# Weight sizes by column sums on TensorE instead of reductions on VectorE, with redrawn scheduling priorities

## The chip, the cores and the metric

The kernel runs on one core of a Trainium2 chip. The metric is the device time of one execution in microseconds; the median of several runs counts. Engines are named as in the profile: PE (TensorE, matmuls), PEld (its weight loads), DVE (VectorE), ACT (ScalarE), POOL (GpSimd), SP (SyncE, which issues all DMAs here).

## The reference

The inputs are a sequence x of 2048 rows and 448 columns, four square weights wq, wk, wv, wo (448x448), w1 (448x1792), w2 (1792x448), a gate vector and 16 values beta. Two branches are mixed row by row:

```python
g = sigmoid((x * gate_w).sum(-1, keepdims=True))
# branch a, 16 heads of 28, 4 segments s of 512 rows, memory M, z from zero
p = softmax(qs @ ks.T * scale + mask); a_dot = p @ vs        # causal in a segment
a_mem = (phi(qs) @ M) / (phi(qs) @ z + 1e-6)                 # phi(t) = t+1 if t>0 else exp(t)
o = sigmoid(beta) * a_mem + (1 - sigmoid(beta)) * a_dot
M = M + phi(ks).T @ vs; z = z + sum(phi(ks))
a = concat(o) @ wo
b = silu(x @ w1) @ w2
out = g * a + (1 - g) * b
```

## The kernel before, in words

**Number formats.** Each operand of a product is split into a high part and the remainder, and three products of parts stand for one. Projections use fp32r parts, everything later f16 parts. To stay in range, f16 operands are multiplied by powers of two that come from the size of a tensor. So the kernel measures sizes: of each segment of x, of wv, of wq and wk, of two 64-column halves of a block of w1 that ride along in the packed wq and wk (HQ, HK), of w1, w2 and wo.

**How a size is taken.** `size` (L378) lets VectorE reduce a loaded piece to one maximum of absolute values for each partition (L385). `scales` (L396) then makes one power of two of them for all partitions: a maximum over the pieces (L411), a transpose on TensorE (L415), a maximum and rounding on one to two rows (L418 to L422), a product with ones on TensorE that spreads it to all partitions (L424), and its reciprocal `up` and the value `top` (L428, L429). For wv, wq and wk a piece is one of four blocks of 128 rows; `weight` (L809) loads it, lets ScalarE write the high part (L817) and VectorE or GpSimd the remainder (L820), and calls `size`: once for wv, twice for wq and wk (the 448 weight columns and the 64 others). The first scale covers the first segment of x and wv together.

**Stages.** First comes the projection stage: for each of 16 groups t (4 segments times 4 groups of heads) a q product and a k product of 11 matmuls each (L561, written mm<-xT,wqs and mm<-xT,wks), for each segment four v products of 11 (sc<-wvs,xT), the memory update (L937, L939) and the retrieval (L974, L975). ScalarE evacuates each product to f16 (`stg`, L853; `vt`, L903) with a factor from the scales, VectorE writes the remainders (L855, L907). For phi ScalarE computes L869 and L871, VectorE L872, ScalarE the high part of phi of q (L876) and VectorE or GpSimd its remainder (L878). Until `scales` has its result, no product can be evacuated. The sizes of w1 and w2 are taken meanwhile by ScalarE (L393). After that, attention (scores L1217, exponentials L1222, PV products L1251) and the first part of the feed-forward products (W1: L561 mm<-xh,wa; W2: L1119) run interleaved; the last stage holds the second part and the products with wo.

**Order.** A scheduler in the kernel, `Sched` (L114), writes all instructions down once, when the program is built. Each task has an engine, an assumed duration, dependencies, buffers from rings, and a priority; the scheduler keeps an assumed clock for each engine and takes the task that can start first, on ties the lowest priority. Constants at the top of the file are these priorities and assumed delays. Engines execute in the order written: an instruction that waits holds up what stands behind it on its engine. PSUM has three rings: three banks for q, k, W1 and W2 products (mm), three for v, scores and wo (sc), two for memory, retrieval, PV and the scales (cc).

## Time and profile before

| | us |
|---|---|
| median of 3 runs | 570.33 |
| lowest and highest run | 569.06, 571.14 |
| the profiled execution | 569.55 |
| its span, first to last instruction | 567.7 |
| mean granted TensorE clock | 0.997 |
| TensorE busy in the span | 546.3 |

A row of a timeline gives the start, the length, engine, line, operation, what is written <- what is read, and in brackets the idle time of the engine before it with the engine that ended it. Rows of equal instructions that follow each other are merged (x4). Matmuls overlap, so a single one's length is longer than its share of the time. In the windows each row is a stage: its bounds, its length, busy time and instructions in the order PE, PEld, DVE, ACT, POOL, the granted clock of TensorE, the share of DMA time and GB/s.

### The profile page before, as it was taken

What the parts mean: (1) busy time and instruction counts of PE and PEld (TensorE: products, weight loads), DVE (VectorE), ACT (ScalarE), POOL (GpSimd) and SP (SyncE); (2) the same over time, 40 slices, a digit from 0 to 9 for tenths busy, and PEclk for the clock granted to TensorE, in tenths of its full rate; (3) what the DMA queues carried; (4) which work ended last, traced back from release to release, by engine and by line L of the source; (5) the groups of instructions that cost most, each with busy time, mean ns of one, the idle gap of its engine ahead of it and who ended that gap; (6) DMA issues with size and microseconds to landing.
All of it is one profiled execution on the core that took longest, in us unless ns stands there. A gap on an engine that the chain in (4) does not pass through costs nothing.

```text
span 567.7 us, 11586 instructions
## 1 busy us (share of the span) xinstructions
PE 546.3 (96%) x4007; PEld 339.8 (60%) x4007; DVE 423.6 (75%) x1097; ACT 400.4 (71%) x695; POOL 359.3 (63%) x501
## 2 busy tenths in 40 slices
PE   8699999999979999999999999999999999999997
PEld 5487788878734455555665555555555655554544
DVE  6999889888778987598865789775888128835644
ACT  6567888875546978889787998878998887203221
POOL 5703636567120578999999998999999993121300
PEclk9999999999989999999999999999999999999999
DMA  8487989986656455522433435364401224699931
GB/s 294 142 229 192 239 232 233 230 216 174 193 170 183 131 148 151 144 72 68 105 112 100 134 95 150 91 174 106 132 5 34 84 66 125 224 228 234 250 98 65
DMA packets 91497, 85.87 MB, mean 151 GB/s; under 512 B 55432, under 2 KB 79112, under 8 KB 91440
## 3 DMA queue, kind: packets, MB, share of 16 engines
q1 hardware_dynamic: 91440, 85.15, 54.5%
q8 instruction: 31, 0.51, 0.4%
q14 instruction: 26, 0.21, 0.1%
HBM read 52.60 MB, written 26.09 MB: 139 GB/s over the span
## 4 chain that ended last, share of the span: by engine, by line
PE 61%; DVE 18%; ACT 9%; DMA 7%; issue 3%; POOL 1%; SPq 0%; DVEq 0%; ACTq 0%; POOLq 0%
PE mm L561 20%; PE mm L1119 19%; PE sc L561 7%; PE sc L1217 5%; PE cc L1251 4%; PE sc L666 4%; DVE sc L676 3%; DVE sizes L385 2%; ACT pf L1222 2%; DMA rawf<-in_w_dram 2%; ACT phl L1234 2%; DMA rawf<-in_x_dram 2%; DMA rwo<-in_wo_dram 1%; DVE stg L855 1%; DVE wb L513 1%
## 5 line engine op out<-in xcount | busy, mean ns | idle before, releaser
L1238 POOL TENSOR_TENSOR phl<-pf,phl 128x384 f16<-128x384 f32 (+1 forms) x192 | 190.0, 1008 | 16.3 <-ACT phl L1234 15.8
L1119 PE MATMUL mm<-wb,ghl 128*128 128x448 f16 (+1 forms) x684 | 147.1, 349 | 0.4 <-DVE ghl L1102 0.2
L561 PE MATMUL mm<-xh,wa 128*128 128x512 f16 x572 | 143.7, 382 | 1.5 <-DVE ghl L1102 1.5
L676 DVE CUSTOM_DVE_ANT_0 sc<-sc,mk 128x384 f32<-128x384 f32 (+1 forms) x192 | 105.2, 572 | 30.3 <-PE sc L666 25.3
L1222 ACT ACTIVATE pf<-sc,es 128x512 f32<-128x512 f32 (+1 forms) x192 | 110.5, 623 | 15.0 <-PE sc L1217 10.3
L1119 PEld LDWEIGHTS <-ghl 128*128 128x128 f16 x684 | 65.1, 97 | 52.8 <-issue 2.3
L561 PEld LDWEIGHTS <-wa 128*128 128x128 f16 x572 | 54.5, 98 | 59.0 <-issue 6.9
L1234 ACT ACTIVATE phl<-pf 128x1280 f16<-128x1280 f32 x64 | 81.4, 1275 | 10.7 <-POOL pf L1228 10.6
L1217 PE MATMUL sc<-ring 86*128 86x512 f16 (+3 forms) x256 | 58.9, 299 | 2.7 <-DVE mx L676 1.5
L666 PE MATMUL sc<-ring 84*128 84x128 f16 (+3 forms) x256 | 57.5, 299 | 0.9 <-DVE mx L676 0.8
L1096 ACT ACTIVATE th<-mm,ths 128x512 f32<-128x512 f32 x52 | 36.2, 698 | 24.5 <-PE mm L561 24.3
L1251 PEld LDWEIGHTS <-phl 128*128 128x128 f16 x1280 | 41.8, 96 | 10.2 <-issue 0.7
L572 POOL TENSOR_TENSOR ol<-ol,ml 128x448 f32<-128x448 f32 x12 | 14.1, 1174 | 51.8 <-DMA ol<-o_scr 28.1
L561 PE MATMUL mm<-xT,wks 128*128 128x512 f32 x176 | 46.0, 399 | 0.8 <-DVE ph L872 0.8
L561 PE MATMUL mm<-xT,wqs 128*128 128x512 f32 x176 | 46.1, 402 | 0.0
L1098 DVE SCALAR_TENSOR_TENSOR mm<-th,mm 128x512 f32<-128x512 f32 x52 | 35.8, 693 | 11.8 <-ACT th L1096 11.5
L1251 PE MATMUL cc<-vg,phl 128*128 128x29 f16 (+1 forms) x1280 | 43.8, 182 | 0.1
L561 PE MATMUL sc<-wvs,xT 128*128 128x450 f32 x176 | 40.0, 374 | 1.9 <-DVE wvs L820 1.0
L1259 DVE TENSOR_REDUCE oraw<-cc 128x116 f32<-128x232 f32 x64 | 25.2, 394 | 21.3 <-PE cc L1251 21.2
L1102 DVE SCALAR_TENSOR_TENSOR ghl<-mm,ghl 128x512 f16<-128x512 f32 x52 | 35.4, 684 | 6.3 <-ACT ghl L1100 6.0
L1100 ACT ACTIVATE ghl<-mm 128x512 f16<-128x512 f32 x52 | 31.1, 605 | 12.2 <-DVE mm L1098 12.2
L1217 PEld LDWEIGHTS <-ring 86*128 86x128 f16 x256 | 24.1, 97 | 22.6 <-issue 2.4
(167 smaller groups left out, 903.0 us busy)
## 6 DMA issues: line engine op xcount, KB each, us to landing
rawf<-in_w_dram SPq DMA_DIRECT2D x26, 256.0 KB
rawf<-in_w_dram SPq DMA_DIRECT2D x28, 224.0 KB
xraw<-in_x_dram SPq DMA_DIRECT2D x16, 256.0 KB
rawf<-in_x_dram SPq DMA_DIRECT2D x16, 256.0 KB
v_scr<-vt SPq DMA_DIRECT2D x16, 232.0 KB
vg<-v_scr SPq DMA_DIRECT2D x16, 232.0 KB
q_scr<-stg SPq DMA_DIRECT2D x16, 224.0 KB
k_scr<-stg SPq DMA_DIRECT2D x16, 224.0 KB
```

The lines of the kernel that those rows point to most:

```text
L561: nc.tensor.matmul(ps(), *p[i], start=(i == 0), stop=(i == n - 1))
L666: nc.tensor.matmul(ps.v[:, u:u + n], rg.v[:KS, 0, hh, i * 128:(i + 1) * 128], rg.v[:KS, 1, hh, :n], start=(i > 0), stop=(i > 0 or j == 3), ...
L676: nc.vector.tensor_tensor_reduce(r, r, MK[:, L - n:], 1.0, NEG, OP.add, OP.max, mx.v[:, hh, i:i + 1])
L1096: e1 = sact(L, lambda ps=ps, th=th: nc.scalar.activation(th.v, ps.v, AF.Tanh, scale=ths[:, s:s + 1]), m, takes=[th], uses=[ps], prio=p0)
L1098: e2 = dve(L, lambda ps=ps, th=th: nc.vector.scalar_tensor_tensor(ps.v, th.v, 1.0, ps.v, op0=OP.add, op1=OP.mult), e1, uses=[ps, th], prio=p0)
L1102: e4 = dve(L, lambda ps=ps, g=g: nc.vector.scalar_tensor_tensor(g.v[:, 1], ps.v, DOWN, g.v[:, 0], op0=OP.mult, op1=OP.subtract), e3, uses= ...
L1119: nc.tensor.matmul(ps.v[:, lo:hi], g.v[:, y, sl], w.v[:, z, lo:hi], start=(j == 0 and i == 0), stop=(j == len(fs) - 1 and i == 2))
L1217: nc.tensor.matmul(ps.v[:, e:e + w], rg.v[:KK, 1, hh, j * 128:(j + 1) * 128], rg.v[:KK, 0, hh, j * 128:], start=True, stop=True)
L1222: ex.append(sact(e, lambda b=b, ps=ps, pf=pf, e=e: nc.scalar.activation(pf.v[:, b, :e], ps.v[:, :e], AF.Exp, scale=es[:, s:s + 1]), m, *ex ...
L1234: hi = copy(1280, lambda hl=hl, flat=flat: nc.scalar.activation(hl.v[:, 0], flat(), AF.Copy), *mk, takes=[hl], uses=[pf], prio=p0 + 2)
L1238: low = pool(w - u, lambda hl=hl, flat=flat, u=u, w=w: nc.gpsimd.tensor_sub(hl.v[:, 1, u:w], flat()[:, u:w], hl.v[:, 0, u:w]), low, uses=[ ...
L1251: nc.tensor.matmul(p[:, i, :2 - z], hl.v[:, z, u:u + 128], vg.v[:, j, hh, :2 - z], start=(z == zs[0] and i == 0), stop=(z == zs[-1] and j ...
```

## The change

For wv, wq and wk the maximum of absolute values is replaced by a bound on it: the largest sum of absolute values over a column, of all 448 rows (and, as the last packed block repeats 64 rows, a bit more). ScalarE writes the absolute values of each block as bf16 (`absw`, a ring of 3), and TensorE multiplies them by a 128x128 matrix of ones, so that four matmuls leave the column sums in one PSUM bank, the same on every partition. VectorE reduces that bank to the largest column and makes the power of two on all partitions at once; the transpose and the spreading product aren't needed for these tensors. The factors change by 2^8 accordingly. The scale of the first segment of x is still made by `scales`, now alone. Some assumed costs (`lo` of a quarter of x, a delay PQL behind phi of q) and some thirty priorities have other values, which rewrites the order of the whole program.

```diff
-HA = 0.2
-HD = 0.18
+HA = 0.22
+HD = 0.14
...
+PQL = 0.23
+AB = 1.77
+PA0 = 1.22
...
-MAXO = 65.18
+MAXO = 68.17
-VS = 5.51
+VS = 7.75
-PVP = 45.12
+PVP = 40.95
-FLO = -11.7
-FHI = 710.96
-WOP = 118.93
+FLO = -8.0
+FHI = 704.93
+WOP = 105.31
...
+    def summed(a, views, ps, ready, prio):
+        n = len(views)
+        def go():
+            for i, v in enumerate(views):
+                w = v()
+                nc.vector.tensor_reduce(sums[:, a + i:a + i + 1], w, axis=(AX.X, AX.XY)[len(w.shape) - 2], op=OP.max)
+            t = sums[:, NS:NS + n]
+            nc.vector.tensor_scalar(t, sums[:, a:a + n], TINY, None, op0=OP.max)
+            nc.vector.tensor_scalar(t.bitcast(I32), t.bitcast(I32), 0x7f800000, None, op0=OP.bitwise_and)
+            nc.vector.tensor_scalar(top[:, a:a + n], t, 1.0 / UP, None, op0=OP.mult)
+            nc.vector.reciprocal(up[:, a:a + n], top[:, a:a + n])
+        t = dve(L + 200 + 400, go, *ready, uses=[ps], prio=prio)
...
     def weight(name, src, prio, places):
+            bank, summing = Buf(BK["cc"]), []
...
-                if name != "v":
-                    j = WQ if name == "q" else WK
...
-                    size(j, lambda w3=w3: w3()[:, :, :GW], D, WLOAD[-1], uses=[b], prio=prio + 0.01 * c)
-                    size(j + 1, lambda w3=w3: w3()[:, :, GW:], 64, WLOAD[-1], uses=[b], prio=prio + 0.01 * c)
+                ab = Buf(R["absw"])
+                t = copy(n, lambda v=v, ab=ab: nc.scalar.activation(ab.v[:, :n], v(), AF.Abs), hi, takes=[ab], uses=[b],
+                         prio=prio + 0.01 * c + AB)
+                t = pe(half(n), lambda c=c, ab=ab: nc.tensor.matmul(bank.v[:, :n], onesb, ab.v[:, :n], start=(c == 0),
+                                                                    stop=(c == NC)), t, t_on2, *summing[-1:],
+                       takes=[] if c else [bank], uses=[ab, bank], prio=prio + PA0)
+                summing.append(t)
...
-                if name == "v":
-                    size(WV, v, n, WS[name][c][1], uses=[b], prio=prio + XS0)
+            if name == "v":
+                summed(WV, [lambda: bank.v[:, :D]], bank, summing[-1:], VC)
+            else:
+                summed(WQ if name == "q" else WK, [lambda: w3()[:, :, :GW], lambda: w3()[:, :, GW:]], bank, summing[-1:],
+                       QS if name == "q" else KS1)
...
-        scales(NSEG - 1, WV + 1, VC)
+        scales(NSEG - 1, NSEG, VC)
         vscale(0, VC)
-        scales(WQ, WQ + 2, QS)
         qscale(0, QS, weigh(WQ, QS))
-        scales(WK, WK + 2, KS1)
         kscale(0, KS1, weigh(WK, KS1, QREADY[0]))
```

More of the change, by code (lines that the diff above doesn't have):

```diff
@@ L44 @@
 TINY = 2.0 ** -40
-WOT = 62.75
+WOT = 66.31
 TUS = 1.6
@@ L49 @@
 HP = 0.18
-HA = 0.2
-HD = 0.18
+HA = 0.22
+HD = 0.14
 HO = 0.09
 HS = 0.14
+PQL = 0.23
+AB = 1.77
+PA0 = 1.22
 SLACK = 0.88
-LOP = 11.31
+LOP = 11.05
 LATE = 0.08
@@ L62 @@
 RB = "cc"
-MP = 12.47
+MP = 13.77
 VF = 2.5
 VA = 1.36
-VS = 5.51
+VS = 7.75
 NV = 8
-XS0 = 2.28
-VC = -7.5
-OT1 = 8.85
-XS = 6.38
-QS = -6.27
-KS1 = -1.14
-SS = 1.1
+XS0 = 2.92
+VC = -6.21
+OT1 = 15.16
+XS = 6.48
+QS = -5.26
+KS1 = -0.83
+SS = 1.72
 def VP(o, k):
     return o + VA + VS * k if o or k > VF else -1.0 + 0.1 * k
-PRICE = 31.16
+PRICE = 27.01
 PVRUNS = [((1, 0), 1)]
-PVP = 45.12
-FLO = -11.7
-FHI = 710.96
-WOP = 118.93
-SZ = 20.35
-SZSTEP = 2.77
-XPRIO = 74.67
-WBP = -20.36
+PVP = 40.95
+FLO = -8.0
+FHI = 704.93
+WOP = 105.31
+SZ = 21.73
+SZSTEP = 2.6
+XPRIO = 83.54
+WBP = -13.06
 XLEAD = 146.82
@@ L334, in infini_mix @@
     cols, at = {}, 0
-    for j, n in enumerate([4] * (NSEG + 5) + [FREE, FB, 4]):
+    for j, n in [(j, 4) for j in range(NSEG)] + [(W1, FREE), (W2, FB), (WO, 4)]:
         cols[j] = (at, at + n)
@@ L339, in infini_mix @@
     most = const.tile([128, NS], F32, name="most")
+    sums = const.tile([128, NS + 2], F32, name="sums")
     top = const.tile([128, NS], F32, name="top")
@@ L342, in infini_mix @@
     oneb = const.tile([NS, 128], BF, name="oneb")
+    onesb = const.tile([128, 128], BF, name="onesb")
     ths = const.tile([128, NSEG], F32, name="ths")
@@ L408, in m1 @@
                 for j in (HQ, HK):
-                    nc.vector.tensor_max(most[:, W1:W1 + 1], most[:, W1:W1 + 1], most[:, j:j + 1])
+                    nc.vector.tensor_max(most[:, W1:W1 + 1], most[:, W1:W1 + 1], sums[:, j:j + 1])
             else:
@@ L433, in scales @@
         return t
+    def summed(a, views, ps, ready, prio):
[10 more added lines that the diff above has]
+        t = dve(L + 200 + 400, go, *ready, uses=[ps], prio=prio)
+        for j in range(a, a + n):
+            SCALED[j] = t
     LATER, GDONE, QREADY, KREADY, END1 = [], [], {}, {}, []
@@ L451, in vscale @@
     def vscale(s, prio, *deps):
-        VREADY[s] = dve(130, lambda: nc.vector.tensor_scalar(sv[:, s:s + 1], up[:, WV:WV + 1], up[:, xi(s)], 2.0 ** -26,
-                                                             op0=OP.mult, op1=OP.mult), SCALED[NSEG - 1 - s], *deps, prio=prio)
+        VREADY[s] = dve(130, lambda: nc.vector.tensor_scalar(sv[:, s:s + 1], up[:, WV:WV + 1], up[:, xi(s)], 2.0 ** -18,
+                                                             op0=OP.mult, op1=OP.mult), SCALED[NSEG - 1 - s], SCALED[WV], *deps, prio=prio)
     def qscale(s, prio, *deps):
-        QREADY[s] = dve(130, lambda: nc.vector.tensor_scalar(sqk[:, s:s + 1], upw[:, 0:1], up[:, xi(s)], 2.0 ** -26,
+        QREADY[s] = dve(130, lambda: nc.vector.tensor_scalar(sqk[:, s:s + 1], upw[:, 0:1], up[:, xi(s)], 2.0 ** -18,
                                                              op0=OP.mult, op1=OP.mult), SCALED[NSEG - 1 - s], *deps, prio=prio)
@@ L461, in go @@
         def go():
-            nc.vector.tensor_scalar(sqk[:, NSEG + s:NSEG + s + 1], upw[:, 1:2], up[:, xi(s)], 2.0 ** -26, op0=OP.mult,
+            nc.vector.tensor_scalar(sqk[:, NSEG + s:NSEG + s + 1], upw[:, 1:2], up[:, xi(s)], 2.0 ** -18, op0=OP.mult,
                                     op1=OP.mult)
             if s < NSEG - 1:
-                nc.vector.tensor_scalar(spk[:, s:s + 1], up[:, WK:WK + 1], up[:, xi(s)], 2.0 ** -25, op0=OP.mult, op1=OP.mult)
+                nc.vector.tensor_scalar(spk[:, s:s + 1], up[:, WK:WK + 1], up[:, xi(s)], 2.0 ** -17, op0=OP.mult, op1=OP.mult)
                 nc.vector.tensor_scalar(spk[:, s:s + 1], spk[:, s:s + 1], UP, None, op0=OP.min)
@@ L478, in go @@
             x = top[:, xi(s)]
-            nc.vector.tensor_scalar(rv[:, s:s + 1], top[:, WV:WV + 1], x, 2.0 ** 26, op0=OP.mult, op1=OP.mult)
+            nc.vector.tensor_scalar(rv[:, s:s + 1], top[:, WV:WV + 1], x, 2.0 ** 18, op0=OP.mult, op1=OP.mult)
             nc.vector.tensor_scalar(omgs[:, s], omg, rv[:, s:s + 1], None, op0=OP.mult)
@@ L486, in scores @@
             x = top[:, xi(s)]
-            nc.vector.tensor_scalar(es[:, NSEG:], top[:, WQ:WQ + 1], x, SCALE * 2.0 ** 52, op0=OP.mult, op1=OP.mult)
+            nc.vector.tensor_scalar(es[:, NSEG:], top[:, WQ:WQ + 1], x, SCALE * 2.0 ** 36, op0=OP.mult, op1=OP.mult)
             nc.vector.tensor_scalar(es[:, s:s + 1], top[:, WK:WK + 1], x, es[:, NSEG:], op0=OP.mult, op1=OP.mult)
@@ L492, in scores @@
                 sl = slice(lo, lo + 64)
-                nc.vector.tensor_scalar(wide[sl, s:s + 1], top[sl, j:j + 1], top[sl, xi(s)], 2.0 ** 26, op0=OP.mult,
+                nc.vector.tensor_scalar(wide[sl, s:s + 1], top[sl, j:j + 1], top[sl, xi(s)], 2.0 ** 18, op0=OP.mult,
                                         op1=OP.mult)
@@ L716, in project @@
         ring("stg", [128, 2, L], F16, 4)
+        ring("absw", [128, L], BF, 3)
         ring("pe", [GW, L], F32, 2)
@@ L746, in project @@
         t_mb = dve(128, lambda: nc.vector.tensor_copy(identb, ident), t_id, prio=-50)
+        t_on2 = pool(128, lambda: nc.gpsimd.memset(onesb, 1.0), prio=-100.5)
         LATER.append(dve(100, lambda: nc.vector.memset(oneb, 1.0), t_mb, prio=-40))
@@ L782, in lo @@
                 nc.vector.tensor_sub(xt.v[REM:128, NC, sl], view()[REM:128, NC], raw(xt.v[REM:128, NC, sl]))
-            XC[0, tb] = [hi, dve(L + 64, lo, hi, uses=[b, xt], prio=prio)]
+            XC[0, tb] = [hi, dve(L + 264, lo, hi, uses=[b, xt], prio=prio)]
             XDONE[0] += XC[0, tb]
@@ L820, in lo, with w3 @@
                     e.tensor_sub(W[name][:, 4 + c], v(), raw(W[name][:, c]))
-                if name != "v":
-                    j = WQ if name == "q" else WK
-                    def w3(v=v):
-                        return v().rearrange("p (g e) -> p g e", g=NG)
-                    size(j, lambda w3=w3: w3()[:, :, :GW], D, WLOAD[-1], uses=[b], prio=prio + 0.01 * c)
-                    size(j + 1, lambda w3=w3: w3()[:, :, GW:], 64, WLOAD[-1], uses=[b], prio=prio + 0.01 * c)
-                WS[name][c] = [hi, dve(D, lambda lo=lo: lo(nc.vector), hi, **k) if name == "v" else either(D, lo, hi, **k)]
-                if name == "v":
-                    size(WV, v, n, WS[name][c][1], uses=[b], prio=prio + XS0)
+                ab = Buf(R["absw"])
[5 more added lines that the diff above has]
+                summing.append(t)
+                WS[name][c] = [hi, dve(D, lambda lo=lo: lo(nc.vector), hi, **k) if name == "v" else either(D, lo, hi, **k)]
+            def w3():
+                return bank.v.rearrange("p (g e) -> p g e", g=NG)
+            if name == "v":
[3 more added lines that the diff above has]
+                       QS if name == "q" else KS1)
         def gates():
@@ L876, in proj @@
                 a = copy(L, lambda: nc.scalar.activation(h2.v[:, 0], ph.v, AF.Copy), tp, takes=[h2], uses=[ph],
-                        prio=prio + 2)
+                        prio=prio + 2, lat=PQL)
                 b = either(L, lambda e: e.tensor_sub(h2.v[:, 1], ph.v, raw(h2.v[:, 0])), a, uses=[ph, h2],
-                        prio=prio + 2)
+                        prio=prio + 2, lat=PQL)
                 PQ[t] = h2, [a, b]
@@ L1054, in project @@
         RDONE.extend(d for n in "vq" for c in WS[n].values() for d in c)
-        RDONE.extend(SIZE[WV] + SIZE[WQ] + SIZE[HQ])
+        RDONE.extend([SCALED[WV], SCALED[WQ]])
         AT[0] = maxima(0, FIRST)
@@ L1291, in outer @@
         nc.vector.tensor_reduce(os[:, 1:2], up[:, :NSEG], axis=AX.X, op=OP.min)
-        nc.vector.tensor_scalar(os[:, 1:2], os[:, 1:2], up[:, WV:WV + 1], DOWN, op0=OP.mult, op1=OP.mult)
-        nc.vector.tensor_scalar(os[:, 2:3], os[:, 0:1], top[:, WV:WV + 1], 2.0 ** 24, op0=OP.mult, op1=OP.mult)
+        nc.vector.tensor_scalar(os[:, 1:2], os[:, 1:2], up[:, WV:WV + 1], 2.0 ** -16, op0=OP.mult, op1=OP.mult)
+        nc.vector.tensor_scalar(os[:, 2:3], os[:, 0:1], top[:, WV:WV + 1], 2.0 ** 16, op0=OP.mult, op1=OP.mult)
         nc.vector.tensor_scalar(os[:, 2:3], os[:, 2:3], top[:, WO:WO + 1], None, op0=OP.mult)
```

## The prediction

> **What bounds the kernel now.** I read the busy totals first, then the windows by stage, then TensorE's waits, then the timeline where those waits are long.

> ```profile
> PE 546.3 (96%) x4007; PEld 339.8 (60%) x4007; DVE 423.6 (75%) x1097; ACT 400.4 (71%) x695; POOL 359.3 (63%) x501
> PE 61%; DVE 18%; ACT 9%; DMA 7%; issue 3%; POOL 1%; SPq 0%; DVEq 0%; ACTq 0%; POOLq 0%
> ```

> TensorE is busy for 96% of the span and carries most of the chain that ended last. The time is its work plus what it stands idle. In the windows, the first two columns are the stage and its length, the third is PE busy, and the one after POOL is the granted clock:

> ```profile
> 0.00:30.00 30.00, 22.73 (x92) 15.36 (x93) 24.50 (x70) 18.65 (x36) 19.84 (x38) 1.00 0.64 216
> 30.00:120.00 90.00, 88.91 (x477) 73.94 (x476) 79.25 (x212) 70.83 (x163) 38.32 (x56) 1.00 0.89 228
> 120.00:170.00 50.00, 46.33 (x237) 34.83 (x236) 40.94 (x108) 27.89 (x51) 22.53 (x34) 0.97 0.65 181
> 170.00:470.00 300.00, 294.45 (x2692) 167.44 (x2691) 221.05 (x613) 253.42 (x401) 260.10 (x356) 1.00 0.39 108
> 470.00:567.70 97.70, 93.83 (x522) 48.24 (x518) 57.89 (x98) 29.63 (x47) 18.54 (x18) 1.00 0.65 178
> ```

> TensorE is idle for 7.3 us of the first 30, 1.1 of the next 90, 3.7 around the end of the projection stage, 5.6 in attention and 3.9 in the last stage. Its longest waits (total, times, longest) have two owners:

> ```profile
> PE cc L415 <- DVE most L411: 3.6, 1, 3.6
> PE cc L974 <- ACT phq L876: 2.6, 1, 2.6
> ...
> PE mm L561 <- DVE ph L872: 0.8, 1, 0.8
> ...
> PE cc L975 <- DVE phq L878: 0.4, 1, 0.4
> ```

> The first is the wait that the change touches. The timeline (start, length) shows VectorE reducing weights and x one after the other until 20 us, while a transpose of the maxima (L415) blocks TensorE's queue:

> ```profile
> 15.51 2.21 DVE L385 TENSOR_REDUCE sizes<-raw 128x1 f32<-128x450 f32 x4
> 17.63 1.86 DVE L385 TENSOR_REDUCE sizes<-xraw 128x1 f32<-128x512 f32 x3
> 19.41 0.61 DVE L385 TENSOR_REDUCE sizes<-raw 128x1 f32<-128x448 f32 x1
> 19.93 0.15 DVE L411 TENSOR_REDUCE most<-sizes 128x2 f32<-128x8 f32 x1
> ```

> ```profile
> 8.91 6.22 PE L561 MATMUL sc<-wvs,xT 128*128 128x450 f32 x29 [0.43 <-DVE wvs L820]
> 14.97 1.53 PE L561 MATMUL mm<-xT,wqs 128*128 128x512 f32 x6
> 20.14 0.27 PE L415 MATMUL cc<-ident,most 128*2 128x128 f32 x1 [3.64 <-DVE most L411]
> ...
> 25.05 1.55 PE L561 MATMUL mm<-xT,wqs 128*128 128x512 f32 x6
> ...
> 39.84 2.66 PE L561 MATMUL mm<-xT,wks 128*128 128x512 f32 x11
> 42.34 2.20 PE L561 MATMUL mm<-xT,wqs 128*128 128x512 f32 x9
> ```

> **The front, part by part.** VectorE loses its 20 reductions of the weights (12 long ones, 2.21/4 = 0.55 us each, and 8 short ones); two of three transposes and broadcasts become one-column ones or go. ScalarE gets 12 absolute values and TensorE 12 column sums (S) of bf16. The order in the built program matters more than the counts: TensorE's first two instructions behind the warm-up are now S of wv's rows 0 and 1, and ten more S stand between projection matmuls (V, Q, K for the products of wv, wq, wk). TensorE takes its queue in order, so the front now hangs on when ScalarE delivers each absolute value. I walk it by hand with paces from rows: a V takes (14.97-8.91)/29 = 0.209 us, a Q or K (42.34-39.84)/11 = 0.228. ScalarE:

> ```profile
> 5.94 2.40 ACT L817 ACTIVATE wvs<-raw 128x450 fp32r<-128x450 f32 x4
> ...
> 27.12 0.62 ACT L393 ACTIVATE rawf<-rawf 128x512 f32<-128x512 f32 x1
> 27.64 0.18 ACT L393 ACTIVATION_READ_ACCUMULATOR rawf<-rawf 128x1 f32 x1
> ```

> An activation of 512 columns lasts 0.62, but the next instruction starts 0.52 behind it; I use 0.52, and estimate 0.47 for 450 columns. (The four wv copies, 0.60 apart, follow their loads.) From 5.94 ScalarE's order then gives the absolute values of wv at 7.0, 8.4, 10.4 and 11.4, of wq at 14.0, 16.0, 17.1 and 17.6, of wk at 18.3, 19.0, 20.1 and 22.7. TensorE: S at 7.05 and 8.45, six V to 9.9, 0.5 idle, S, three V, S at 11.4, eleven V to 13.95, S, eleven V to 16.5, S, two V, S, three Q, S, eight Q and three K to 20.95, three S, six K to 23.0, S, two K: at 23.65 it has 33 V, 11 Q and 11 K behind it. Before, it has the same behind it at 25.05, where the second Q group starts. So 1.4 us are gained, the S included: at the pace of the bf16 or f16 row

> ```profile
> 188.81 1.89 PE L561 MATMUL mm<-xh,wa 128*128 128x512 f16 x8
> ```

> twelve S cost at most 12 x 0.236 = 2.8; they lie in the former wait. I take 0.215 each, the last one's latency off.

> From there to the first memory group the new order has 11 V, 33 Q and 25 K, 15.5 us of work. The fifth Q or K group needs the PSUM bank of the first K, whose last reader on VectorE ends at about 30.7 by the same walk (VectorE's 512-column operations 0.60 apart, 17.63 above), 1.0 us after TensorE gets there: so 40.15. Before, TensorE has 61 V, 33 Q and 33 K done at 42.34; 17 V less and 14 Q or K more put the same work at 42.34-3.55+3.19 = 41.98. **The front gains 1.8 us.** If activations were paced at their full 0.62, the same walk ends at 44.1, 2.1 us late: these are my bounds, and I stay with the row of the starts.

> **The rest of the projection.** Counted in the built program's order with the paces above, the redrawn order keeps as much TensorE work between a product and its use as before (least between K and its memory group 11.2 us, formerly 11.4; least between a product and its bank's next turn 6.1, formerly 5.0), so I leave the 1.1 us idle at 30 to 120 as they are; they could go or double. VectorE's relief is worth nothing there, because TensorE hardly waits.

> **The end of the stage.** Before, the last K group met a bank not yet read (0.8), and the last retrieval then waited 2.55 for the phi of q and 0.35 for its remainder, 3.7 in all:

> ```profile
> 156.09 0.62 ACT L871 ACTIVATE pe<-pr 112x512 f32<-112x512 f32 x1
> 156.85 0.69 ACT L853 ACTIVATE stg<-mm,sqk 128x512 f16<-128x512 f32 x1
> 158.69 0.63 ACT L876 ACTIVATE phq<-ph 112x512 fp32r<-112x512 f32 x1 [1.15 <-DVE ph L872]
> ```

> There two weight casts stood ahead of that exponential on ScalarE. In the new order they stand ahead of the whole group, and the bank has 8.5 us instead of 5.0, so that wait goes. The retrieval again stands right behind the last K; its phi must still wait on ScalarE behind K's own evacuation. From the end of K: 0.2 to the evacuation, 0.55 for it, 0.65 for phi, 0.05 back: 1.45 idle; and 0.5 more for the remainder on VectorE, which stands behind K's. 1.95 instead of 3.7: **1.7 gained**, by these rows between 0 and 3.

> ```profile
> 160.00:165.00 5.00, 4.91 (x19) 2.36 (x20) 3.37 (x18) 1.36 (x2) 2.52 (x5) 0.66 0.36 102
> ```

> Right behind that wait the granted clock was 0.66 for 5 us: 5 x 0.34 = **1.7 lost**. With 1.95 idle I expect it not to drop, with doubt: in the front 3.64 idle cost no clock (1.00 above), here 2.9 with a short burst between did. [...]

> **Attention and the last stage.** Their instructions are the same but for a few that change between VectorE and GpSimd. TensorE's work between a head's scores and its PV products is 9.7 us on average (formerly 10.1), least 7.2 in both, and with 7.2 PV waited for 0.1 us in all:

> ```profile
> L1251 PE MATMUL cc<-vg,phl 128*128 128x29 f16 (+1 forms) x1280 | 43.8, 182 | 0.1
> ```

> I cost it at nothing; the cover is that work. Without it a head waits by what it lacks.

> **Sum.** 567.7 - 1.8 - 1.7 - 1.7 = 562.5; the profiled execution took 569.55, 1.85 more than its span: 564.35. It was 0.78 under the median of 570.33, so the median would be 565.1.

> **The rivals.** (1) The clock drops all the same: 566.8. For it: the stall is still at the same place; against: it is shorter. (2) ScalarE delivers at 0.62 each, so the front loses 2.1 where I let it gain 1.8: 565.1 + 3.9 = 569.0. For it: ScalarE is now asked for all but a little of the first 27 us; against: the two starts 0.52 apart. In this case the change doesn't do what it says: TensorE waits for ScalarE instead of VectorE. (3) Slower: the attention order's thinner cover. 34 of 64 heads lose cover, 50 us together. If a fifth of it becomes waiting, 10 us come on top: 575. It eats the whole gain from a tenth (5 us) on. For it: POOL, which feeds PV, is busy 260 of the 300 us there; against: the least cover is unchanged. (4) The new order halves the 5.6 us that TensorE idles in attention: 562.3.

> **How the numbers follow.** A measurement of this kernel can tell about 0.5%, 2.85 us, from no change: faster is below 567.5, slower above 573.2. Forecast 0.42 (563 to 567.4); clock 0.15, of which two thirds come out under 567.5; ScalarE 0.20, a quarter of it under that; cover 0.13, all slower; less idle 0.10. Faster 0.42+0.10+0.10+0.05 = 0.67, which I lower to 0.64 for an unseen wait between 45 and 150 us; same 0.22, slower 0.14. The range 561.5 to 571.5 takes in (4), (1) and (2) and leaves out (3) and the tails.

> **What would show it.** In the new profile, TensorE's wait for L411's maxima is gone and no wait for an absolute value is above 0.6; the second Q group starts near 23.7 and the first memory group near 40. The last retrieval waits about 1.5 and then 0.5, the W1 products start near 157.4 (now 160.9) and the clock behind them is 1.00. Idle time from there on is within 2 us of 9.5. I am wrong if ScalarE's activations in the first 20 us start 0.6 apart, or if PV's products show waits of over 5 us.

## The result, and the profile after

The changed kernel takes **572.12 us** (median of 16 runs, 568.74 to 573.86); the kernel before took 569.64 in the same comparison (16 runs, 567.36 to 571.39). The ratio is **1.0038, 95% interval 1.002 to 1.0056**: a little slower, less than the 0.5% that the prediction wanted for a verdict, but not faster. Predicted was 565.1. The profiled execution of the changed kernel took 573.86, with a span of 571.9 and a mean clock of 0.987 (before: 569.55, 567.7 and 0.997). It is the slowest of the 16; the mean clock over all 16 is 0.991, so the two profiles show more difference in the clock than there is on average.

The busy totals and the chain by engine, after:

```profile
PE 550.8 (96%) x4015; PEld 343.1 (60%) x4015; DVE 425.6 (74%) x1083; ACT 406.7 (71%) x707; POOL 355.3 (62%) x499
PE 71%; DVE 11%; ACT 7%; POOL 4%; DMA 4%; issue 3%; SPq 0%; DVEq 0%; POOLq 0%; ACTq 0%
```

TensorE's idle time hardly changed: 571.9 - 550.8 = 21.1 us, before 567.7 - 546.3 = 21.4. What grew is its **busy** time, by 4.5 us. The windows by stage (columns as before) show where:

```profile
0.00:30.00 30.00, 23.20 (x92) 15.48 (x93) 23.80 (x58) 21.91 (x46) 19.85 (x39) 0.97 0.68 228
30.00:120.00 90.00, 89.59 (x485) 75.21 (x485) 81.03 (x211) 71.89 (x164) 34.94 (x53) 0.99 0.84 225
120.00:170.00 50.00, 47.46 (x236) 35.81 (x236) 40.66 (x107) 28.21 (x52) 20.32 (x34) 0.97 0.67 186
170.00:470.00 300.00, 292.26 (x2643) 165.80 (x2642) 221.03 (x609) 252.54 (x396) 254.57 (x350) 0.99 0.39 106
470.00:571.90 101.90, 98.33 (x566) 50.83 (x564) 59.03 (x100) 32.14 (x51) 25.61 (x25) 0.99 0.64 175
```

The clock column has changed: 0.97 in the front and 0.99 in attention, where it was 1.00. Idle time is 6.8, 0.4, 2.5, 7.7 and 3.6 us (before 7.3, 1.1, 3.7, 5.6, 3.9): the front's idle time fell by 0.5 and attention's grew by 2.2. W1 starts at 160.95, before at 160.93; so nothing was gained up to there, and the 4.2 us that this execution is longer come behind it. TensorE's longest waits (total, times, longest):

```profile
PE cc L850 <- ACT absw L848: 5.3, 4, 2.9
...
PE sc L689 <- DVE mx L694: 2.0, 1, 2.0
...
PE cc L1006 <- ACT phq L908: 1.3, 1, 1.3
PE cc L1007 <- DVE phq L910: 1.1, 2, 0.6
```

The 3.6 us for the maxima are down to 0.45 (the size of x's first segment, at 17.00). In their place stand 5.3 for absolute values (one of 2.9) and a new 2.0 in the row maxima of attention.

**The wait in the front.** The timeline of the changed kernel (start, length):

```profile
21.73 0.42 DVE L450 TENSOR_SCALAR sums<-sums 128x2 f32<-128x2 f32 x1
22.05 3.78 POOL L823 TENSOR_TENSOR xT<-xraw,xT 128x512 fp32r<-128x512 f32 x3
...
22.18 1.22 DVE L451 TENSOR_SCALAR sums<-sums 128x2 int32<-128x2 int32 x1
23.44 1.19 DVE L452 TENSOR_SCALAR top<-sums 128x2 f32<-128x2 f32 x1
...
24.74 0.19 DVE L475 TENSOR_SCALAR sv<-up 128x1 f32<-128x1 f32 x1
...
24.97 1.16 ACT L935 ACTIVATE vt<-sc,sv 128x448 f16<-128x448 f32 x2 [4.01 <-DVE sv L475]
...
26.70 0.38 PE L850 MATMUL cc<-absw,onesb 128*128 128x512 bf16 x1 [2.87 <-ACT absw L848]
```

Two steps on two columns take 1.2 us each, and each ends just behind one of GpSimd's three subtractions (22.05 + 3.78/3 = 23.31 and 24.57): by these times VectorE is held until GpSimd's subtraction ends. So the factor sv comes at 24.74, ScalarE stands 4.01 us in front of the evacuation that needs it, the last absolute value of wk stands behind that evacuation, and TensorE waits 2.87 for it.

**The wait in attention** has the same shape with another step:

```profile
348.30 2.89 POOL L1268 TENSOR_TENSOR phl<-pf,phl 128x384 f16<-128x384 f32 x3
...
348.96 2.98 DVE L707 TENSOR_SCALAR mx<-mx,lift 128x16 f32<-128x16 f32 x1
...
351.40 0.51 POOL L1258 TENSOR_SCALAR_AFFINE_SELECT pf<-pf 128x384 f32<-128x384 f32 x1
...
354.08 0.68 DVE L694 TENSOR_REDUCE mx<-sc 128x4 f32<-128x512 f32 x1
...
354.81 0.82 PE L689 MATMUL sc<-ring 84*128 84x256 f16 x4 [2.03 <-DVE mx L694]
```

The subtraction of the lift, 0.31 us in the median of its 16 instances, takes 2.98 here, to 351.94, when GpSimd's unbroken run ends (351.91); the maxima that free TensorE's bank stand behind it.

**The clock.** In each of the 20 profiled executions the clock's changes lie on a grid: here the clock falls to 0.50 at 28.1, 161.2, 188.5 and 355.8 us, which are 39, 8 and 49 times 3.413 us apart, and stands there for one cell of 3.41 us each time. Windows laid on that grid, each cell in front of a change and the one behind it (third column PE busy, clock the one after POOL):

```profile
24.71:28.12 3.41, 1.42 (x7) 1.17 (x7) 3.38 (x9) 3.15 (x6) 1.11 (x1) 1.00 0.07 28
28.12:31.54 3.42, 3.42 (x10) 2.68 (x9) 3.25 (x12) 2.49 (x7) 1.28 (x1) 0.50 0.56 194
157.83:161.24 3.41, 1.62 (x11) 1.20 (x11) 2.15 (x4) 2.43 (x4) 1.02 (x2) 1.00 0.70 207
161.24:164.66 3.42, 3.42 (x10) 1.23 (x9) 2.93 (x18) 0.00 (x0) 1.45 (x3) 0.50 0.21 61
185.13:188.54 3.41, 1.99 (x9) 0.86 (x9) 3.41 (x11) 3.41 (x6) 1.20 (x2) 1.00 0.82 230
188.54:191.95 3.41, 3.41 (x13) 1.49 (x11) 1.71 (x2) 2.24 (x5) 3.22 (x5) 0.50 0.73 177
352.39:355.80 3.41, 1.31 (x7) 0.57 (x6) 3.41 (x8) 2.92 (x5) 1.09 (x2) 1.00 0.47 110
355.80:359.22 3.42, 3.42 (x11) 1.48 (x10) 3.35 (x12) 3.21 (x5) 3.34 (x6) 0.50 0.32 104
```

Each cell in which TensorE is idle for 1.4 to 2.1 of 3.41 us is followed here by one at half clock (0.50), which by these rows costs up to 3.41/2 = 1.7 us of work, an estimate. The execution before has one such pair ahead of its last matmuls (161.5 us), this one four. The least idle time with a half clock behind it was 1.42 us here (185.13 to 188.54), under half a cell.

### The profile page after: what moved, and what is told of

Same layout as the page of the kernel before. It is cut to its first block, busy times and chain, and to the rows that moved or that the text cites. A ratio compares the mean times of both kernels' runs of the same rounds, so it can differ in the third digit from the quotient of the medians.

```text
span 571.9 us, 11602 instructions
## 1 busy us (share of the span) xinstructions
PE 550.8 (96%) x4015; PEld 343.1 (60%) x4015; DVE 425.6 (74%) x1083; ACT 406.7 (71%) x707; POOL 355.3 (62%) x499
## 4 chain that ended last, share of the span: by engine, by line
PE 71%; DVE 11%; ACT 7%; POOL 4%; DMA 4%; issue 3%; SPq 0%; DVEq 0%; POOLq 0%; ACTq 0%
PE mm L584 27%; PE mm L1149 20%; PE sc L584 8%; PE sc L1247 5%; PE cc L1281 4%; PE sc L689 4%; DVE sc L699 3%; DMA rawf<-in_x_dram 2%; ACT phl L1264 1%; POOL phl L1268 1%; ACT absw L848 1%; ACT pf L1252 1%; DVE ghl L1132 1%; DMA xraw<-in_x_dram 1%; DMA rawf<-in_w_dram 1%
## 5 line engine op out<-in xcount | busy, mean ns | idle before, releaser
L584 PE MATMUL mm<-xh,wa 128*128 128x512 f16 x572 | 143.6, 385 | 1.1 <-DVE ghl L1132 0.9
L584 PEld LDWEIGHTS <-wa 128*128 128x128 f16 x572 | 54.5, 98 | 58.6 <-issue 6.8
L1247 PE MATMUL sc<-ring 86*128 86x512 f16 (+3 forms) x256 | 60.1, 300 | 3.9 <-DVE mx L699 2.1
L689 PE MATMUL sc<-ring 84*128 84x128 f16 (+3 forms) x256 | 55.2, 301 | 2.8 <-DVE mx L694 2.0
L584 PE MATMUL mm<-xT,wqs 128*128 128x512 f32 x176 | 47.8, 412 | 0.0
L584 PE MATMUL mm<-xT,wks 128*128 128x512 f32 x176 | 47.5, 401 | 0.0
L584 PE MATMUL sc<-wvs,xT 128*128 128x450 f32 x176 | 40.3, 373 | 0.0
L601 ACT ACTIVATE oh<-ol,os 128x448 f16<-128x448 f32 x16 | 10.6, 664 | 39.0 <-POOL ol L595 39.0
```

Source lines behind the costliest of these rows:

```text
L584: nc.tensor.matmul(ps(), *p[i], start=(i == 0), stop=(i == n - 1))
L689: nc.tensor.matmul(ps.v[:, u:u + n], rg.v[:KS, 0, hh, i * 128:(i + 1) * 128], rg.v[:KS, 1, hh, :n], start=(i > 0), stop=(i > 0 or j == 3), ...
L1247: nc.tensor.matmul(ps.v[:, e:e + w], rg.v[:KK, 1, hh, j * 128:(j + 1) * 128], rg.v[:KK, 0, hh, j * 128:], start=True, stop=True)
```

## The experiments

**Theories.** A: short steps of VectorE held by GpSimd are what the change loses, through late factors in the front and the 2.0 us wait in attention. B: the order that the new constants draw is worse by itself. C: the column sums cost TensorE time that is not hidden. Ratios below are to the kernel before on the same chip, with 95% intervals.

### Each part alone

**New constants alone, and column sums alone.**

```diff
 e4: kernel before, with all constants of the change
 e3: changed kernel, with all constants of before (HA, HD ... XPRIO, WBP)
```

> The sizes by VectorE as before, with the priorities and assumed delays of the changed kernel. If the priorities cost the time: ratio 1.003 to 1.01, with attention idle near 7.7 us. If the column sums cost it: ratio 0.997 to 1.002 and attention idle near 5.6.

> Column sums, but every priority and assumed delay that the kernel before has is set to its value there. If the column sums cost the time: ratio 1.003 to 1.01, with TensorE waiting for absolute values for 3 us or more. If the redrawn priorities cost it: ratio 0.995 to 1.001, and attention idle within 1 us of the kernel before (5.6).

Measured: new constants alone 571.06, **1.0036 (1.0017 to 1.0055)**, as much as the whole change. Column sums in the old order 581.75, 1.0232 (1.0202 to 1.0262). So the column sums in their own order net nothing, and the loss sits in the constants, or both parts lose and gain in ways that cancel.

### The front (theory A)

**One column at a time in the column sums' steps.**

```diff
-            t = sums[:, NS:NS + n]
-            nc.vector.tensor_scalar(t, sums[:, a:a + n], TINY, None, op0=OP.max)
...
+            for i in range(n):
+                t, j = sums[:, NS + i:NS + i + 1], slice(a + i, a + i + 1)
+                nc.vector.tensor_scalar(t, sums[:, j], TINY, None, op0=OP.max)
... (the other three steps likewise)
```

> The four small steps of the power of two are written for one column at a time; the order of all else is that of the changed kernel. Theory (two-column f32 steps of VectorE wait for GpSimd's running instruction, and that lateness passes through ScalarE's queue to TensorE): each step takes 0.13 to 0.2 us instead of 0.4 to 1.2, the factor of v is ready near 23.3 instead of 24.9, TensorE's wait for the last absolute value falls from 2.9 to 1.6 or less, and the half clock behind it mostly goes; ratio to the kernel before 0.997 to 1.001. Rival (ScalarE's twelve absolute values are late by themselves): nothing moves, wait 2.9, ratio 1.004.

Measured: 571.34, 1.0051 (1.003 to 1.0072). The steps fall to 0.14 to 0.16 us each, sv comes at 22.88, the longest wait for an absolute value is 1.0 and the front keeps its clock. But TensorE's waits show the place taken by a bank, and the time is not better:

```profile
PE cc L851 <- ACT absw L849: 2.3, 3, 1.0
...
PE sc L690 <- DVE mx L695: 2.0, 1, 2.0
PE mm L585 <- DVE stg L888: 1.9, 1, 1.9
```

Nor is the front free of held steps. Right behind sv a step on one column, but with two tensors, now ends with GpSimd's second subtraction (22.07 + 2 x 3.76/3 = 24.58):

```profile
22.07 3.76 POOL L824 TENSOR_TENSOR xT<-xraw,xT 128x512 fp32r<-128x512 f32 x3
...
23.23 1.38 DVE L469 SCALAR_TENSOR_TENSOR upw<-up,own,upw 128x1 f32<-128x1 f32 x1
```

So e1 doesn't test a front without any hold.

**A fourth buffer for the absolute values.**

```diff
-        ring("absw", [128, L], BF, 3)
+        ring("absw", [128, L], BF, 4)
```

> Four buffers for absolute values instead of three, so that the last one of wk stands ahead of the v evacuations on ScalarE. Theory (the last absolute value is late only because it stands behind evacuations that wait for the late factor of v): TensorE's wait for it falls below 0.3 us although the factor stays late, the wait moves in part to the PSUM banks of the next products, and the front is 1 to 3 us shorter; ratio 0.996 to 1.002. Rival (ScalarE's load): the wait stays within 1 us of 2.9, ratio 1.004.

Measured: 573.61, 1.0083 (1.0053 to 1.0114). The wait for absolute values falls to 2.0, and 3.3 us of waiting for a bank (L584 <- stg L887) come in its place. My reading, not tested further: with the further buffer TensorE runs ahead to the product whose bank waits for the late factor.

**Two-tensor forms.** Against the hold, the lift's subtraction alone (e6), or it and the gates' 128x16 steps together with e1's one-column steps (e7), became operations on two tensors from SBUF.

```diff
-nc.vector.tensor_scalar(mx.v, mx.v, lift[:, s:s + 1], None, op0=OP.subtract)
+nc.vector.scalar_tensor_tensor(mx.v, mx.v, 1.0, lift[:, s:s + 1, None].to_broadcast([128, 4, TB]),
+                               op0=OP.mult, op1=OP.subtract)
```

> The changed kernel with one instruction written in another form: the row maxima's subtraction of the lift (128x16, 16 times) as an operation with two tensors from SBUF instead of one tensor and a scalar per partition; every engine's order stays. Theory A (that step waits for GpSimd's subtractions): its 16 instances take 0.25 to 0.35 us each, none over 0.5; the 2.0 us wait of TensorE near 355 us falls under 0.6, the half-clock window behind it goes, and the time is 2 to 3.7 us under the changed kernel's 572.1: 568.4 to 570. Theory B (late order): the wait stays over 1.5 us, since the queue in front of it is late whatever this step takes: 571.5 to 572.5. Theory C (the step is held in every form, as both operands come from SBUF): one instance still takes over 1 us, time unchanged.

> The changed kernel with one column at a time in the column sums' steps, and with the lift's subtraction and the three 128x16 steps of the gates written with two tensors from SBUF. Theory A (VectorE's short steps held by GpSimd's subtractions are what the change costs): the two gate steps at 20 us take under 0.4 instead of 1.30 and 0.94, the factor sv comes before 22.5 us instead of 24.74, no wait of TensorE over 1.2 us in 5 to 60 us, none over 1 us at 355, clock of 0.99 or more, and 564.5 to 567.5 us, faster than the kernel before by 0.2 to 0.6 per cent. Theory B (the order written by the new constants is worse by itself): 570 to 571, as with one column alone, because the waits for banks and for ScalarE take the place.

Measured: e6 571.37, 1.0053 (1.0028 to 1.0077); e7 571.52, 1.0046 (1.0024 to 1.0069). The form frees nothing: e7's gate steps still take 1.30 and 0.93 us, and a subtraction up to 1.12 in both. In these two profiled executions it was let in after one of GpSimd's subtractions, and the 2.0 us wait was 0.5; over all their runs the mean clock, 0.991, is still that of the changed kernel. With the new constants alone and the same form (e11, below) it was held in full:

```profile
343.97 2.90 POOL L1239 TENSOR_TENSOR phl<-pf,phl 128x384 f16<-128x384 f32 x3
...
344.64 2.97 DVE L684 SCALAR_TENSOR_TENSOR mx<-mx,lift 128x16 f32<-128x16 f32 x1
...
347.06 0.52 POOL L1229 TENSOR_SCALAR_AFFINE_SELECT pf<-pf 128x384 f32<-128x384 f32 x1
```

It ends at 344.64 + 2.97 = 347.61, as GpSimd's unbroken run does (347.06 + 0.52 = 347.58): with two tensors the step was held for 2.97 us, with a scalar operand in the changed kernel for 2.98. The kernel before with e7's forms:

> The kernel before with the lift's subtraction and the gates' 128x16 steps written with two tensors from SBUF; order unchanged. Theory A: there the longest instance of the subtraction takes 1.26 us and no wait of TensorE over 1 us comes from it, so the cover holds: within 0.3 per cent of the kernel before. If it is faster by over 0.4 per cent, the same holding costs the kernel before as well, and what the changed kernel with the same forms gains is no gain of its column sums.

Measured: 569.07, 0.9999 (0.9978 to 1.0019): unchanged.

### What the sizes are worth, and what the sums cost (theory C)

**Scales given.** The sizes of the three weights, and all that takes them, replaced by constants at the start, under the new and under the old constants:

```diff
+        def given():
+            for j, v in ((WV, 1.0), (WQ, 128.0), (HQ, 1.0), (WK, 128.0), (HK, 1.0)):
+                nc.vector.memset(top[:, j:j + 1], v / UP)
+                nc.vector.memset(up[:, j:j + 1], UP / v)
...
(e9 leaves out absw, its column sums and summed(...); e12, with its own values, size(...) and scales(...) of the weights)
```

> The changed kernel without the sizes of wv, wq and wk: absolute values, column sums and the steps behind them are left out, and their scales are written as constants at the start (right for this data only). It is the most that any way of taking these sizes could give under the new constants. Theory A (late sizes and the waits around them in the front are what the change loses): no wait of TensorE over 1.2 us in 6 to 60 us, the second half of the projection starts 3 us or more earlier, W1 begins before 158 us, and 565 to 567 us. Theory B (the order drawn by the new constants sets the time, whatever the front does): 569 to 571.

> The kernel before, with the scales of wv, wq and wk written as constants (right for this data only) instead of taken by VectorE: what the sizes cost there in all, the 3.6 us wait for the maxima among it. If the front's waits show in the end: 564 to 566 us. If the rest of the order takes the gain back (banks, ScalarE, or a wait at the end of the projection stage): 568 to 569.

Measured: 567.33, 0.9966 (0.9948 to 0.9984), and 567.86, 0.9965 (0.9949 to 0.998). That is all there was to win: **0.35%, 2.0 us**, against the kernel before. Under the new constants VectorE's sizes cost 0.70% (1.0036 to 0.9966) and the column sums, with all that hangs on them, 0.72% (1.0038 to 0.9966): one is as dear as the other. The wait for the maxima stays, 3.3 and 4.2 us, because the same transpose also needs the size of x's first segment.

**The matmuls put back, unread**: in the front (e10), and all twelve behind the fourth memory group (e16; meant for about 50 us, they ran at 63.1 to 65.4).

```diff
+                t = pe(half(n), lambda c=c: nc.tensor.matmul(
+                    bank.v[:, :L], onesb, onesb[:, None, :].to_broadcast([128, 4, 128]), start=(c == 0), stop=(c == NC)),
+                    hi, t_on2, *summing[-1:], takes=[] if c else [bank], uses=[bank], prio=prio + PA0)
(e16: prio=60.0)
```

> As the run with given scales, but TensorE still makes the twelve column-sum matmuls, on a constant tile, each after its chunk's rounded copy; nobody reads them. The difference to the run with given scales is the price of the twelve matmuls on TensorE alone. Theory C (TensorE is the bound, so they cost their own time, 12 by 0.21 us): 2 to 3 us slower than with given scales. Theory A (they lie in gaps of the front, where TensorE has some 5 us idle before 20 us): under 1 us slower.

> Given scales and the twelve unread matmuls, as before, but all twelve at about 50 us, behind the fourth memory group, where TensorE has no gaps; the order of the front is that of the run with given scales alone (567.3 us). Theory C (they cost their own time on an engine that is the bound): 567.3 + 12 by 0.21 = 569.9, within 0.8. Theory D (in the front they cost more, since groups that other engines wait for come later): also near 570, and so the 571.8 of the run with them in the front holds some 2 us of delay. Theory E (in the front part of them lies in gaps, and the 4.5 us came from elsewhere, the clock or a bank): 571 to 572 here as well.

Measured: e10 571.84, **1.0047** (1.0024 to 1.0069); e16 569.89, **1.0009** (0.9988 to 1.003); without them 0.9966. Late they cost 0.43%, 2.4 us, about their own time. In the front they cost 0.81%, 4.6 us, though TensorE is idle for about 5 us there: its idle time in the first 30 us is 5.8 with them and 4.7 without. The groups of TensorE's rows, e16 and then e10:

```profile
L855 PE MATMUL cc<-onesb 128*128 128x512 bf16 x12 | 2.8, 380 | 0.0
```

```profile
L855 PE MATMUL cc<-onesb 128*128 128x512 bf16 x12 | 4.5, 447 | 0.0
L421 PE MATMUL cc<-ident,most 128*1 128x128 f32 x5 | 1.5, 292 | 4.7 <-DVE most L417 4.7
```

In the order with the twelve, 20 v products stand ahead of the transpose that blocks the queue, without them 31; so TensorE waits 4.7 instead of 3.3 at it, and the 13 v products that could fill the gap stand behind it. This is e10's order: in the changed kernel that transpose waits 0.45 us and the sums wait 5.3 for absolute values, so the 4.6 us are the price in e10, and the split in the changed kernel isn't shown.

**x's first size given too** (e12's edit, with `(NSEG - 1, 0.25)` added and its `size` and `scales` left out).

> The kernel before with the scales of wv, wq, wk and of x's first segment all written as constants (right for this data only), so that the front waits for no size at all. Theory F (the wait for the maxima, 4.2 us with the weights' scales given, is that for x's first segment, and it was the front's real bound): no such wait, W1 3 to 4 us earlier than 157.7, 563 to 565 us. Theory G (behind that wait the same place waits for something else: the rounded weights, the low parts made by VectorE and GpSimd, a bank): 567 to 568, as with the weights' scales given.

Measured: 568.65, 0.9993 (0.997 to 1.0017). The wait is gone, TensorE is busy 26.8 of the first 30 us (e12: 23.5), and the gain is given back at 47 us, where the size of the next segment is late because its data are:

```profile
45.55 0.69 DVE L385 TENSOR_REDUCE sizes<-xraw 128x1 f32<-128x512 f32 x1 [3.67 <-DMA xraw<-in_x_dram]
...
47.07 0.16 PE L424 MATMUL cc<-diag,oneb 1*128 1x1 bf16 x1 [3.22 <-DVE diag L422]
```

### What the new constants lose (theories A and B)

**The late constants put back** (MAXO, WOT, LOP, PRICE, PVP, FLO, FHI, WOP, WBP as before).

> The changed kernel with nine of its constants, those that set the order of the rest of the work (the row maxima, the output projection, the loads of its weights), put back to what they were before; the order of the first 60 us and the column sums stay. Theory A (the 2.98 us step of VectorE at 349 us, which waits for GpSimd's subtractions, makes the 2.0 us wait at 355 and the half clock behind it): with another order around 350 us the step meets another moment of GpSimd, no single wait of over 1.5 us in 200 to 450 us, and 569 to 570 us. Theory B (the new late order is worse by itself): 568 to 569, the idle time of TensorE in 170 to 470 us back at 5.6. Theory C (the loss is set in the front, where the wait of 2.87 us stands): still 572, with whatever late order.

Measured: 573.54, 1.0076 (1.0052 to 1.01). The 2.0 us wait is gone in the profiled execution, but TensorE is idle for 8.6 us from 170 to 470 us (changed kernel 7.7). It speaks against both A's and B's number, and C's 572 is the nearest: the old late order is no remedy behind the new front.

**The subtraction in the other form, and on ScalarE**, both with the new constants and VectorE's sizes.

```diff
-f0 = dve(100, lambda: nc.vector.tensor_scalar(mx.v, mx.v, lift[:, s:s + 1], None, op0=OP.subtract), ...
+f0 = act(16, lambda: nc.scalar.activation(mx.v, mx.v, AF.Identity, bias=lift[:, NSEG + s:NSEG + s + 1]), ...
     (e13; lift[:, NSEG + s] holds -lift, one more short step per segment; e11: the two-tensor form above)
```

> The kernel before with the new constants (VectorE takes the sizes as before), and the lift's subtraction in the form with two tensors from SBUF. The same constants without that form gave a mean clock of 0.988 and 571.1 us, a wait of 2.0 us near 351 us. Theory A (the long subtraction makes that wait, and the wait the half clock): the wait is under 0.6, the mean clock 0.991 or more, and the time 568 to 569.5, as the kernel before. Theory B (the late order itself): 570.5 to 571.5 with a clock still near 0.988.

> The kernel before with the new constants (VectorE takes the sizes), and the lift's subtraction on ScalarE instead of VectorE. Theory A (VectorE held by GpSimd's subtractions makes the 2.0 us wait near 350 us and the half clock behind it): the wait is under 0.6, the mean clock over 0.990 against 0.988, and 568.3 to 569.5. Theory B (the late order itself): the wait stays over 1.5 or comes from another line; 570.3 to 571.

Measured: e11 570.34, 1.0025 (1.0005 to 1.0045), held as shown above. e13 569.47, **1.0000 (0.9983 to 1.0017)**. On ScalarE the 16 subtractions take 0.31 us each in the mean (of e17 below, which has the same edit), the 2.0 us wait is gone, and the two stretches at 350 us that were half idle and then half clocked with the new constants alone (1.39 of 3.41 busy, then a clock of 0.51) are full:

```profile
347.69:351.10 3.41, 3.41 (x20) 1.77 (x19) 3.38 (x9) 3.12 (x6) 3.41 (x6) 1.00 0.83 248
351.10:354.52 3.42, 3.42 (x42) 2.31 (x40) 2.60 (x7) 2.75 (x6) 3.42 (x5) 1.00 0.07 22
```

**The same in the changed kernel.**

> The changed kernel, column sums and all, with the lift's subtraction on ScalarE instead of VectorE. With the new constants alone this took the ratio from 1.0036 to 1.0000. Theory A+C (the loss is the sum of the held subtraction, some 2 us, and of the column sums' matmuls against the sizes' worth, near zero or a little over): the 2.0 us wait near 355 us goes, 569.5 to 570.5, ratio 1.000 to 1.002. Theory C alone (with the column sums the wait costs nothing more, as two runs without it suggest, at 1.005): 571 to 572.

Measured: 568.69, **0.9995 (0.9979 to 1.0011)**. One step moved takes back the whole loss, with the front and its 2.87 us wait as they were. The gain is clock: the mean over its runs is 0.996, against 0.991 in the runs of the changed kernel, while span times clock, the time at full clock, is the same (564.6 and 564.9). The scheduler wrote the order around the moved step anew in e13 and e17, so part of the gain may be that order's; the runs don't separate it.

That wait and the clock do go together: in 8 of the 20 profiled executions a wait of 1.9 to 2.0 us stands at this step, each of the eight has a half-clock cell right behind it, beginning at 351 to 357 us, and none of the other twelve has one there.

**Loss by work and loss by clock.** The same two means, over all runs, part the loss (an estimate, since it takes TensorE as the bound all along). The kernel before has 562.2 to 562.8 us at full clock and mean clocks of 0.991 to 0.993 in its five sets of runs. The new constants alone have 562.0 and 0.988: they lose by the clock. The changed kernel has 564.9 and 0.991: on average it loses 2.1 to 2.7 us by work and idle time at full clock, about what the twelve matmuls cost in e16, and at most 0.7 us by the clock (0.0012 of 570). So moving the step doesn't remove what the column sums added; it lifts the clock above that of the kernel before.

### A version without work for TensorE

**The sizes of wv by ScalarE's accumulator**, in the kernel before (e15), and with the new constants and e13's edit (e18).

```diff
-                    size(WV, v, n, WS[name][c][1], uses=[b], prio=prio + XS0)
+                    total(WV, v, n, WS[name][c][1], uses=[b], prio=prio + XS0)
```

> The kernel before, with the four sizes of wv taken by ScalarE's accumulator (sums along the free axis instead of VectorE's maxima) in place of VectorE's reductions; no work is added to TensorE. The sizes of all three weights are worth 1.4 to 2 us in all; this takes 2.3 us off VectorE and puts 4 by 0.80 us on ScalarE. Theory A (VectorE's queue sets the wait for the maxima): the wait falls from 3.6 to under 2.5 and 568 to 569 us. Theory B (x's own size is what comes last): the wait unchanged, and the time that of the kernel before within 0.2 per cent.

> The new constants, VectorE's sizes for wq and wk, the sizes of wv by ScalarE's accumulator, and the lift's subtraction on ScalarE: nothing added to TensorE, the held step gone. Theory A+C: 567.5 to 568.8, 0.1 to 0.3 per cent under the kernel before, which would beat both kernels. Rival (the wait for the maxima moves to another line, as it did with the weights' scales given): within 0.1 per cent of the kernel before.

Measured: e15 568.55, 0.9994 (0.9977 to 1.0011); its wait for the maxima is 2.0 instead of 3.6, but the projection stage ends no earlier (W1 at 159.80; two other executions of the old order 159.26 and 160.93). e18 **565.61, 0.9942 (0.9919 to 0.9965)**: faster than both kernels, and 2 us below the range expected. Its two parts alone gave nothing (0.9994 and 1.0000); why they give 0.6% together isn't shown. Its busy totals and first two stages:

```profile
PE 547.0 (97%) x4007; PEld 341.9 (61%) x4007; DVE 418.8 (74%) x1084; ACT 404.2 (72%) x719; POOL 355.4 (63%) x496
```

```profile
0.00:30.00 30.00, 25.56 (x97) 17.32 (x98) 24.52 (x69) 19.55 (x44) 19.50 (x38) 0.94 0.71 236
30.00:120.00 90.00, 89.85 (x490) 75.17 (x489) 81.02 (x228) 72.95 (x167) 40.94 (x62) 1.00 0.88 227
```

TensorE is 4.4 us idle in the first 30 and starts W1 at 156.44, and no cell at 350 us is half clocked. The accumulator puts about 4 by 0.57 + 0.19 us on ScalarE, an estimate from the kernel before, which takes the sizes of w2 in this way (0.57 for an activation of 448 columns, 0.19 for reading the accumulator).

## Why the prediction was wrong, point by point

**The front's 1.8 us: failed.** The walk held to the fifth S (13.95 predicted, 13.93 measured) and, on ScalarE, to the eleventh absolute value (20.1, 19.92). It had no term for the transpose of x's own maxima, which waits 0.45 us; the three K that it let end at 20.95 ended at about 21.6:

```profile
17.00 0.27 PE L421 MATMUL cc<-ident,most 128*1 128x128 f32 x1 [0.45 <-DVE most L417]
...
20.93 0.85 PE L584 MATMUL mm<-xT,wks 128*128 128x512 f32 x3
21.63 0.82 PE L850 MATMUL cc<-absw,onesb 128*128 128x512 bf16 x3
```

It then had the last absolute value at 22.7. That one came at 26.65, behind the late factor sv, since VectorE's steps on two columns took 0.42, 1.22 and 1.19 us instead of about 0.15, held by GpSimd. The second Q group started at 27.38 instead of 23.7, the first memory group at 44.42 instead of 40.15. By the prediction's own count the kernel before has the same work behind it at 41.98, so up to there the front lost 2.4 us instead of gaining 1.8; 1.7 of them can be the half-clock cell at 28.12. Whether this is why the kernel lost isn't shown: with those steps unheld (e1) it is no faster, but there another step is held. The step that failed for the time as a whole is the value put on the column sums themselves. I let twelve of them lie in the former wait and so priced them at nothing beyond the front's walk. The runs show that VectorE's sizes cost 0.70% under the new constants (1.0036 to 0.9966) and the column sums that replace them 0.72% (1.0038 to 0.9966), most of it the twelve matmuls (0.43% late, 0.81% in e10's front); what ScalarE's absolute values and VectorE's steps add can't be told from nothing (1.0047 to 1.0038).

**Rest of the projection: right**, 0.4 us idle at 30 to 120 us, 1.1 before.

**End of the stage: right in the waits, wrong in the clock.** 1.45 + 0.5 predicted, 1.30 and 0.49 measured. I expected no clock drop, since 3.64 us idle in the front had none. The half clock came all the same (my first rival): a cell at 0.50, so the 1.7 us counted as gained were not. On the grid the comparison was void: the 3.64 were split into 1.7 and 2.0 over two cells, and the 1.79 lay in one. Of 39 cells idle for 40 to 60%, 34 were followed by half clock (last section), so by these counts a drop was likely, and the two of the front were the exception.

**Attention at nothing: failed.** I looked at the work between scores and PV, and waits there stayed small: the row maxima lost 2.0 us, at a step of VectorE that the trace of before already showed at up to 1.26 us against a median of 0.33 (the three times are the shortest, the median and the longest in ns):

```profile
L684 DVE TENSOR_SCALAR mx<-mx,lift x16: 234/330/1256, 105.2 to 440.1; 128x16 f32<-128x16 f32 x16
```

My third rival had the stage right and the place and mechanism wrong, and its 10 us were far too much. In place of "nothing" stand 2.2 us more idle time in the profiled execution and the half-clock cell behind the wait. The new constants alone lose 0.36%, 2.0 us, over all stages, and that goes when the step leaves VectorE (1.0036 to 1.0000; the change 1.0038 to 0.9995). That this term alone decided the sign isn't shown: by the full-clock times above, what the changed kernel has over the kernel before is about the column sums' own price.

**The second rival** (absolute values paced at 0.62) was wrong in its mechanism: they followed each other at the pace of the starts until the late factor stopped ScalarE.

What stays open: why e5 loses with the old late order; why e6 and e7, whose profiled executions have no 2.0 us wait, are no faster (whether the step was held in their other executions is not on record); how much of e13's and e17's gain is the new order around the moved step; and why e18's two parts give more together than alone.

## What to carry to other kernels

Work moved onto the engine that bounds the kernel can cost its own time and more even beside idle gaps, as the twelve matmuls did (2.4 us in e16, behind the front; 4.6 in e10's front, where the longest wait, 4.7 us, ended only when the maxima came); price the prize first, by the same kernel with the value given (4.0 us to win here under the new constants, 2.0 against the kernel before, and 4.1 paid for the column sums). Look for a short step whose longest instance is many times its median (2.98 us against 0.31 here): it may be held by another engine, and a redrawn order can put it where a wait hangs on it. And count idle time by cells of the clock's grid, 3.413 us in these traces, not by single waits.

## What the runs showed of the hardware

```profile
24.92:28.34 3.42, 1.56 (x7) 1.31 (x7) 3.38 (x9) 3.29 (x7) 0.97 (x1) 1.00 0.11 40
28.34:31.75 3.41, 3.02 (x14) 2.26 (x12) 3.24 (x12) 2.92 (x8) 1.29 (x1) 1.00 0.77 249
```

So where idle time falls in a cell can make a difference of up to 1.7 us for each such place, half a cell, an estimate. The changed kernel's fastest run (568.74) had a clock of 0.997, its slowest (573.86) 0.987.
